# A linear-attention and long-convolution kernel: the filter's spectrum made straight on frequency partitions, one form of inverse tile, and a new order of all steps

## The chip, the cores and the metric

The kernel runs on one core of one Trainium2 chip. Its time is the device time of one execution in microseconds; the runs shown are three, and their median counts. A profile of one more execution shows where the time goes on the engines: PE (TensorE matmuls) and PEld (its weight loads), DVE (VectorE), ACT (ScalarE), POOL (GpSimd), SP (SyncE, which here only issues DMAs), and the DMA engines.

## The reference

Two parts follow each other. The first is linear attention with a feature map of exponentials, for 8 batches and 8 heads of 576 positions and width 64; the second takes its output, laid out as 8 x 576 x 512, projects it three ways, convolves one of the three with a filter along the sequence by FFT, multiplies, and projects once more.

```python
def phi(x):
    proj = np.einsum('bhsd,df->bhsf', x, w_phi)              # 64 -> 128 features
    proj = proj - np.max(np.abs(proj), axis=-1, keepdims=True)
    return np.concatenate([np.exp(proj), np.exp(-proj)], axis=-1)
q_p, k_p = phi(q), phi(k)
kv = np.einsum('bhsf,bhsd->bhfd', k_p, v)
z = np.sum(k_p, axis=2)
num = np.einsum('bhsf,bhfd->bhsd', q_p, kv)
den = np.einsum('bhsf,bhf->bhs', q_p, z)[..., None] + 1e-06
x = (num / den)                                              # then [8, 576, 512]

proj = x @ w_proj                                            # 512 -> 3 x 512
x1, x2, x3 = proj[..., :D], proj[..., D:2*D], proj[..., 2*D:]
X2 = np.fft.rfft(x2, n=576, axis=1)
H = np.fft.rfft(filter_fft, n=576, axis=0)[None]
y = x1 * np.fft.irfft(X2 * H, n=576, axis=1) * x3
out = y @ w_out
```

## The kernel before

All eight batches pass through the same chain of small steps, and every step is one method of a class. The order in which instructions are issued is written out by hand: the string `PLAN` (lines 31 to 193) is a list of words such as `Ie,0,2@2`; `run` (line 1061) walks through it and calls for each word the method of that name with the arguments that follow, and `@2` gives the PSUM bank (one of eight banks of 512 fp32 columns) that the step uses. Each engine executes its own instructions in the order of the list and waits for what they need; in the same way SP's and POOL's queues take their DMA issues in this order. Where a step has more than one possible engine, the word names it (`DVE`, `ACT`, `POOL`). `RING` gives how many buffers a tile has in turn.

The steps of one batch b, with v or m counting its four tiles:

- `load` (line 589) brings k, q and v of a batch into SBUF from POOL's queue; `trh` (601) transposes k and q by DMA from SP's queue. For batch 0, `loadh`, `pt` and `pte` do it by halves with PE. `w_load` (571) brings the weights, w_proj in three pieces.
- `Pk`, `Qn`, `Pkt`, `Qnt` (626 to 652): projections by w_phi; `maxk`, `maxq` and the like: their largest magnitude on DVE. `mhi`, `mlo`, `trm`, `trme` transpose the maxima of q.
- `ex`, `exkt`, `exqt` (685): exponentials on ACT; `Pq`: projection of q less its maximum; `em`, `vs` (742, 747): v scaled by the exponential of the maximum of k, mostly on POOL.
- `KV`, `KVe` (753): the sums over positions; `NE`, `rc`, `xn`, `NEt`, `rct`, `xnt` (771 to 813): numerator, denominator and quotient. `trx`, `trxt` (815): the quotient transposed by DMA from SP's queue into xT (for batch 0 three tiles go by PE, `ptx`).
- The forward transform of x runs before its projection: `f1`, `f2` (844, 850) fold the positions by sums and differences on DVE or POOL (both inputs in SBUF), `F` (855) multiplies by the tables D and Dt, `Fe` evicts into XF, `Xl` copies the last frequencies. `X2` (892) projects the spectrum, and `Y1` (899) multiplies it by the filter's spectrum in HTe, HTo and H5. `m3` (909) adds two of the products.
- `X1`, `X3` (940, 952): the other two projections, from xT; `X1e` evicts the first on ACT or DVE, `tm` (958) multiplies the second onto it on DVE.
- The inverse transform has two forms. `I` (966) makes even and odd halves with three matmuls each, in two banks; `Ie` (989) copies the even half to SBUF (es) on ACT, `Ip` and `Im` (999, 1002) form sum and difference on DVE (cv), and `ym` (1037) multiplies by x1s on POOL or DVE. `J` (1021) makes both final halves directly with five matmuls each, for which the table inv holds four more rows (`gen_neg`, `gen_ends`), and `yj` (1030) multiplies on DVE straight from PSUM. Of the 32 tiles 21 are made by I, 11 by J.
- `O` (1046): the output projection from yT, whose first step needs all four products of its batch; `Oe` (1052) evicts on ACT or DVE into one of four o buffers, `st` (1055) stores each in two halves, nearly always from SP's queue.

The filter's spectrum is made once, at the start, out of fl (512 rows, loaded in eight pieces) and flt (the 64 rows left): `fa` folds once on POOL in fp32, `rev` (497) reverses the partitions of two of the four results by an fp32 matmul with a reversed identity, `fb` (501) folds again on DVE into bf16, `Ff` (506) multiplies by D and Dt for each of four column blocks, with positions on the contraction side and channels on the partitions, `Ffe` scales and evicts, `Hl` gathers the last frequencies on ACT, `H` (532) turns the result by matmuls with the identity so that frequencies stand on the partitions, and `He` (538) evicts with signs and halves into HTe, HTo and H5. The copy `ft` is written for POOL, but the helper `copy` (293) knows only ACT and DVE and gives it to DVE.

`wz` (311) is a filler: two matmuls of zeros, 128 x 512, into a free bank. The list has ten of them, all ahead of the first X1.

`late` (275) closes the scratch space of the start, and the tiles T0 to T4, es, cv, yT and o are laid out in its place.

## Time and profile before

| | |
|---|---|
| median of three runs | 310.7 us (308.33 to 312.73) |
| span of the profiled execution | 311.6 us, the time used for it below |
| PE busy | 281.0 us, 90% |
| DVE busy | 268.6 us, 86% |
| ACT busy | 216.3 us, 69% |
| POOL busy | 203.8 us, 65% |
| mean granted clock of TensorE | 0.974 |
| read from and written to HBM | 33.75 MB, 9.44 MB |

The page gives no time around the span; the profiled execution is one among runs that lie between 308.33 and 312.73 us. In the rows, a line such as "L972 PE MATMUL" names the line of the code, the engine and the operation; "x126" is a count, and behind the bar stand the busy time of the group in us, the mean duration of one in ns, and the idle time of the engine ahead of the group with what ended it. Matmuls overlap in their pipeline, so that the duration of one is longer than the distance from one to the next; the chain of waits shows the latter (start, us, what).

### The profile page before, as it was taken

What the parts mean: (1) busy time and instruction counts of PE and PEld (TensorE: products, weight loads), DVE (VectorE), ACT (ScalarE), POOL (GpSimd) and SP (SyncE); (2) the same over time, 40 slices, a digit from 0 to 9 for tenths busy, and PEclk for the clock granted to TensorE, in tenths of its full rate; (3) what the DMA queues carried; (4) which work ended last, traced back from release to release, by engine and by line L of the source; (5) the groups of instructions that cost most, each with busy time, mean ns of one, the idle gap of its engine ahead of it and who ended that gap; (6) DMA issues with size and microseconds to landing.
All of it is one profiled execution on the core that took longest, in us unless ns stands there. A gap on an engine that the chain in (4) does not pass through costs nothing.

```text
span 311.6 us, 10240 instructions
## 1 busy us (share of the span) xinstructions
PE 281.0 (90%) x4331; PEld 205.3 (66%) x4360; DVE 268.6 (86%) x447; ACT 216.3 (69%) x345; POOL 203.8 (65%) x163
## 2 busy tenths in 40 slices
PE   1968977999999996999899799999999999999992
...
GB/s 162 235 203 159 136 202 193 105 190 133 91 164 204 94 110 170 116 160 107 114 198 82 131 160 153 172 175 160 84 117 4 56 93 69 19 110 21 1 115 192
DMA packets 72735, 40.20 MB, mean 129 GB/s; under 512 B 53040, under 2 KB 67504, under 8 KB 72688
## 3 DMA queue, kind: packets, MB, share of 16 engines
...
HBM read 33.75 MB, written 9.44 MB: 139 GB/s over the span
## 4 chain that ended last, share of the span: by engine, by line
PE 70%; DVE 12%; DMA 7%; ACT 5%; issue 3%; SPq 1%; POOL 0%; DVEq 0%; POOLq 0%
PE ps L919 16%; PE ps L897 10%; PE ps L1049 8%; PE ps L764 5%; PE ps L972 4%; PE ps L778 4%; DMA xT<-xn 4%; DMA out_dram<-o 3%; PE ps L1028 3%; PE ps L858 3%; PE ps L862 3%; PE ps L928 2%; DVE mq L707 2%; PE ps L665 2%; PE ps L638 2%
## 5 line engine op out<-in xcount | busy, mean ns | idle before, releaser
L919 PE MATMUL ps<-xT,wproj 128*128 128x256 bf16 x512 | 65.8, 275 | 4.3 <-DVE x1s L960 2.3
L919 PEld LDWEIGHTS <-wproj 128*128 128x128 bf16 x512 | 48.6, 98 | 14.5 <-issue 5.1
L707 DVE TENSOR_REDUCE mk<-ps 128x8 f32<-128x1024 f32 (+1 forms) x40 | 44.0, 1110 | 5.9 <-ACT HTo L295 2.2
L707 DVE TENSOR_REDUCE mq<-ps 128x8 f32<-128x1024 f32 (+1 forms) x40 | 44.0, 1110 | 5.5 <-PE ps L638 4.5
L749 POOL TENSOR_TENSOR vm<-vn,vm 128x1152 bf16<-128x1152 bf16 x14 | 30.4, 2178 | 18.2 <-ACT vm L743 18.2
L749 POOL TENSOR_TENSOR vp<-vn,vp 128x1152 bf16<-128x1152 bf16 x16 | 34.8, 2180 | 10.5 <-ACT vp L743 10.3
L911 POOL TENSOR_TENSOR T<-T,T 128x1024 bf16<-128x1024 bf16 x12 | 25.5, 2124 | 21.9 <-DVE T L907 21.8
L693 ACT ACTIVATE Ekp<-ps 128x1024 bf16<-128x1024 f32 x32 | 32.8, 1030 | 6.6 <-DVE mk L707 3.3
L1038 POOL TENSOR_TENSOR yT<-cv,x1s 128x576 bf16<-128x576 f32 x19 | 24.3, 1289 | 18.3 <-DVE x1s L964 12.8
L852 POOL TENSOR_TENSOR xf<-SD 128x512 bf16<-128x512 bf16 x27 | 31.2, 1170 | 6.7 <-DVE SD L846 5.3
L693 ACT ACTIVATE Ekm<-ps 128x1024 bf16<-128x1024 f32 x32 | 32.8, 1033 | 3.6 <-DVE mk L707 2.7
L693 ACT ACTIVATE Eqm<-ps 128x1024 bf16<-128x1024 f32 x32 | 32.9, 1034 | 3.1 <-PE ps L671 2.9
L1049 PE MATMUL ps<-wout,yT 128*128 128x512 bf16 x133 | 34.3, 385 | 0.7 <-issue 0.2
L693 ACT ACTIVATE Eqp<-ps 128x1024 bf16<-128x1024 f32 x32 | 32.5, 1031 | 3.4 <-PE ps L671 3.3
L846 POOL TENSOR_TENSOR SD<-xn 128x512 bf16<-128x512 bf16 x23 | 26.5, 1160 | 12.6 <-DVE xn L797 12.6
L897 PE MATMUL ps<-wproj,XF 128*128 128x512 bf16 x117 | 30.3, 380 | 0.7 <-issue 0.2
L295 ACT CAST x1s<-ps 128x512 bf16<-128x512 f32 (+1 forms) x30 | 16.0, 548 | 13.1 <-PE ps L928 8.4
L797 DVE TENSOR_TENSOR xn<-ps,r 128x512 bf16<-128x512 f32 x32 | 22.0, 689 | 1.1
L1049 PEld LDWEIGHTS <-yT 128*128 128x128 bf16 x144 | 13.4, 99 | 14.1 <-issue 0.6
L990 ACT COPY es<-ps 128x288 f32<-128x288 f32 x21 | 8.5, 404 | 20.3 <-PE ps L972 19.8
L960 DVE TENSOR_TENSOR x1s<-ps,x1s 128x512 bf16<-128x512 f32 x32 | 21.7, 683 | 0.6 <-ACT x1s L295 0.4
L778 PE MATMUL ps<-KVs,Eqp 128*128 128x65 bf16 x256 | 19.6, 192 | 2.2 <-DVE mq L707 0.6
...
## 6 DMA issues: line engine op xcount, KB each, us to landing
...
vn<-in_v_dram POOLq DMA_DIRECT2D x8, 576.0 KB, 7.5
kn<-in_k_dram POOLq DMA_DIRECT2D x7, 576.0 KB, 9.7
qn<-in_q_dram POOLq DMA_DIRECT2D x7, 576.0 KB, 6.6
wproj<-in_moe_w_proj_dram POOLq DMA_DIRECT2D x3, 512.0 KB, 5.9
...
```

Source lines behind the costliest of these rows:

```text
L693: self.nc.scalar.activation(e, p, AF.Exp, bias=0.0, scale=1.0 if g == "p" else -1.0)
L707: self.nc.vector.tensor_reduce(out=out, in_=src, axis=AX.X, op=ALU.max, apply_absolute_value=True)
L749: self.eng(eng).tensor_tensor(out=t[:, :, :, 0:64], in0=self.at("vn", b)[:, 2 * X:2 * X + 2], in1=t[:, :, :, 64:65].to_broadcast([128, 2, ...
L778: self.mm(self.pb(u, 65 * a, 65 * a + 65), E, KVs[:, u, v, s, :], start=(s == 0), stop=(s == 1))
L797: self.nc.vector.tensor_tensor(out=o, in0=n[:, :, :, 0:64], in1=self.at("r", 4 * b + v).to_broadcast([128, 2, 4, 64]), op=ALU.mult)
L846: self.eng(eng).tensor_tensor(out=o[:, :, 2 * i:2 * i + 2, :], in0=x[:, :, 0:2, :], in1=x[:, :, 2:4, :], op=ALU.subtract if i else ALU.add)
L852: self.eng(eng).tensor_tensor(out=o[:, :, 2 * i:2 * i + 2, :], in0=x[:, :, 0:4:2, :], in1=x[:, :, 1:4:2, :], op=ALU.subtract if i else ALU ...
L897: self.mm(self.pb(0), l, w[:, kt, 512:1024], start=(kt == 0), stop=(kt == 3))
L911: self.eng(eng).tensor_tensor(out=Y, in0=Y, in1=self.at(f"T{2 * e + 1}", b), op=ALU.add)
L919: self.mm(o[:, d], w[:, kt, f0 + 128 * m:f0 + 128 * m + 128], y[:, 1, ::-1, ::-1] if d else y[:, 0], start=(kt == 0), stop=(kt == 3))
L1038: self.eng(eng).tensor_tensor(out=self.at("yT", b)[:, m, 0:SEQ], in0=self.turn_of("cv", (b, m)).rearrange("p x h t -> p (x h t)"), in1=sel ...
L1049: self.mm(self.pb(0), y[:, kt, 128 * c:128 * c + 128], w[:, kt, :], start=(kt == 0), stop=(kt == 3))
```

## The change

What is computed stays the same. Five things differ.

1. **Filter spectrum.** `fa` now writes its folded rows in bf16 and nothing is reversed or folded a second time. Instead the table D gets a partner with reversed partitions, D2: `rv` multiplies D by a reversed identity in bf16 (two matmuls of 288 columns), and `rve` evicts it in two parts on DVE, one with the sign changed. `Hd` (in place of Ff, Ffe, Hl and H) makes each of the five tiles of the spectrum directly with frequencies on the partitions: three matmuls of 512 columns for each of four tiles, five for the last, whose tables zl2 and zlt are gathered by `zl` with ten small copies on POOL (over zeros that `zm` sets). `He` now also applies the scale HS.
2. **Inverse tiles.** `J`, `yj`, `gen_neg` and `gen_ends` are gone; all 32 tiles go by `I`, `Ie`, `Ip`, `Im` and `ym`. The table inv has 6 rows in place of 10. es and cv have three buffers in place of two.
3. **Engines.** Some steps change their engine, by the words of the list (steps before and after):

| step | before | after |
|---|---|---|
| f2 | DVE 5, POOL 27 | DVE 13, POOL 19 |
| f1 | DVE 9, POOL 23 | DVE 11, POOL 21 |
| ym | DVE 2, POOL 19 (and 11 yj on DVE) | DVE 4, POOL 28 |
| Fe | DVE 6, ACT 26 | DVE 11, ACT 21 |
| Oe | DVE 17, ACT 19 | DVE 9, ACT 27 |
| KVe | DVE 6, ACT 10 | DVE 9, ACT 7 |
| X1e | DVE 8, ACT 24 | DVE 5, ACT 27 |
| m3 | DVE 4, POOL 12 | DVE 3, POOL 13 |

4. **Order.** The whole list is written anew. Among other things the loads of q and k of batch 1 and their transposes come ahead of the load of v of batch 0, v of batch 1 and k of batch 2 ahead of the third piece of w_proj, and the filter's 64 rows (`fl_loadt`) behind the transposes of batch 1.
5. **Zero matmuls.** The method `wz` and its ten words stay; seven now stand at the head of the list, one ahead of `rv`, one in batch 2 and one between batches 2 and 4.

The diff, with most of the list left out:

```diff
@@ -24,172 +24,177 @@
 
 RING = {'Ekp': 4, 'Ekm': 4, 'Eqp': 3, 'Eqm': 3, 'vp': 3, 'vm': 3, 'r': 4, 'o': 4, 'kn': 2, 'qn': 2,
         'vn': 2, 'kT': 2, 'qT': 2, 'mk': 2, 'mq': 2, 'mh': 2, 'mT': 2, 'xT': 2, 'xTt': 2, 'KVs': 2,
-        'Fkp': 2, 'Fkm': 2, 'Fqp': 2, 'Fqm': 2, 'rt': 2, 'xnt': 2, 'es': 2, 'cv': 2, 'yT': 2}
+        'Fkp': 2, 'Fkm': 2, 'Fqp': 2, 'Fqm': 2, 'rt': 2, 'xnt': 2, 'es': 3, 'cv': 3, 'yT': 2}
 
 
 
 PLAN = """
-fl_load,2,1 cols_h loadh,q,0,0 zeros fl_load,3,0 gi_part loadh,q,0,1 ident fl_load,0,0 cols_i
-fl_load,1,0 gi_nr loadh,k,0,0 fl_load,1,1 w_load,phi loadh,k,0,1 cols_f load,v,0 fl_loadt ang,2
-gi_fr fl_load,0,1 gz,DVE ang,3 wz,10@0 fl_load,2,0 load,k,1 fl_load,3,1 wz,26@1 load,q,1 frac,3
-pt,q,0,0,0@0 gi_back ang,1 sin,3 pt,q,0,0,1@1 cols_m pte,DVE,q,0,0,0@0 ang,0 wz,13@2
...
+gi_part w_load,phi gz,DVE cols_h cols_i zeros fl_load,0,0 cols_f fl_load,2,0 wz,27@1 fl_load,0,1
+loadh,q,0,0 ident back,ACT wz,13@5 loadh,k,0,1 gi_nr loadh,q,0,1 wz,20@1 ang,3 wz,25@5 loadh,k,0,0
+fl_load,3,0 frac,3 fl_load,3,1 fl_load,1,0 ang,2 gi_fr wz,9@6 fl_load,2,1 ang,1 load,q,1
+fl_load,1,1 wz,1@1 wz,12@0 frac,2 pt,q,0,0,0@3 sin,3 trh,q,1,0 pt,q,0,0,1@0 pte,ACT,q,0,0,0@3
+trh,q,1,1 load,k,1 trh,k,1,1 trh,k,1,0 pte,ACT,q,0,0,1@0 zm,POOL cols_m frac,1 pt,k,0,1,0@2 sin,2
+ang,0 w_phi pt,k,0,1,1@3 Qn,0,1@4 sin,1 frac,0 pt,q,0,1,1@0 sin,0 Qn,0,0@6 load,v,0 pt,q,0,1,0@1
+pte,DVE,k,0,1,0@2 pte,ACT,k,0,1,1@3 maxq,0,1@4 fa,POOL,0 Pk,0,2@2 pt,k,0,0,0@4 pte,DVE,q,0,1,1@0
+pte,ACT,q,0,1,0@1 maxq,0,0@6 Qn,0,2@0 load,v,1 pt,k,0,0,1@5 Qn,0,3@6 pte,DVE,k,0,0,0@4 maxq,0,2@0
+Pk,0,0@0 pte,DVE,k,0,0,1@5 ex,k,p,0,2@2 maxq,0,3@6 ex,k,m,0,2@2 Qnt,0@4 ex,k,p,0,0@0 w_load,proj,2
+maxk,0,2@2 Pk,0,3@6 ex,k,m,0,0@0 ex,k,p,0,3@6 Pkt,0@2 exkt,m,0@2 maxqt,0@4 w_load,proj,1 mhi,0
+maxk,0,0@0 mlo,POOL,0 Pk,0,1@4 ex,k,m,0,3@6 exkt,p,0@2 maxk,0,1@4 maxk,0,3@6 ex,k,p,0,1@4
+maxkt,0@2 wz,10@0 rv@0 ex,k,m,0,1@4 load,k,2 one trm,0@7 trme,ACT,0@7 em,m,0,1 em,p,0,0
+rve,DVE,1@0 w_load,proj,0 em,m,0,0 fa,POOL,1 Pq,0,1@4 rve,DVE,0@0 Qn,1,0@2 em,p,0,1 vs,POOL,m,0,0
+fl_loadt Qn,1,3@0 ex,q,p,0,1@4 vs,DVE,p,0,0 Pq,0,3@6 ex,q,m,0,1@4 ex,q,p,0,3@6 vs,POOL,p,0,1
...
+xn,2,0@4 m3,POOL,1,1 exqt,p,2@2 Pq,2,3@0 Xl,DVE,1 f1,DVE,2,0,0 Pk,3,1@2 X2,1,4@4 KVe,DVE,2,1@6
+NE,2,2@6 maxk,3,1@2 wz,14@5 ex,q,m,2,3@0 f1,DVE,2,0,1 rc,2,2@6 ex,q,p,2,3@0 ex,k,p,3,1@2
...
+Pk,3,2@4 Ie,1,1@2 Pk,3,0@0 Im,1,1@2 ym,POOL,1,2 Ip,1,1@2 ym,POOL,1,3 ym,POOL,1,1 maxk,3,0@0
+ex,k,p,3,2@4 ex,k,m,3,2@4 X1,2,0@7 f1,POOL,2,1,1 maxk,3,2@4 X1,2,2@2 X1t,2@3 trh,q,4,0 X1,2,1@6
+st,SP,0,2,0 X1e,ACT,2,2@2 X1e,ACT,2,0@7 yt,ACT,1 ex,k,m,3,0@0 X1e,ACT,2,1@6 ex,k,p,3,0@0 Qn,3,3@4
+trh,q,4,1 X1te,DVE,2@3 f2,POOL,2,0,0 O,1,0@2 X3,2,0@3 Oe,ACT,1,0@2 O,1,4@7 maxq,3,3@4 em,p,3,0
+tm,2,0@3 Qnt,3@5 st,SP,0,0,0 Oe,ACT,1,4@7 Qn,3,1@3 f2,POOL,2,1,0 em,m,3,0 Pk,3,3@0 f2,DVE,2,1,1
...
+Ie,2,0@4 Ip,2,3@0 Im,2,3@0 st,SP,1,4,0 Ip,2,1@6 f1,POOL,3,1,0 ym,POOL,2,2 wz,26@0 Qn,4,1@0
...
+ym,POOL,7,0 Ie,7,1@4 Ie,7,2@0 ym,DVE,7,3 O,6,3@2 Ip,7,1@4 Ip,7,2@0 Im,7,1@4 ym,POOL,7,1
+st,SP,5,3,0 Oe,ACT,6,3@2 st,SP,6,3,1 st,SP,6,3,0 Im,7,2@0 O,6,0@4 Oe,ACT,6,0@4 st,SP,6,0,1
+st,SP,6,0,0 X3,7,2@0 tm,7,2@0 ym,DVE,7,2 O,6,1@6 Oe,ACT,6,1@6 O,7,2@2 yt,ACT,7 Oe,ACT,7,2@2
+O,7,4@4 Oe,DVE,7,4@4 st,SP,6,1,0 O,7,3@1 st,SP,6,1,1 st,SP,7,2,1 st,ACT,7,2,0 O,7,0@0 st,SP,7,4,1
+Oe,DVE,7,3@1 O,7,1@4 st,SP,7,3,0 st,ACT,7,4,0 Oe,DVE,7,0@0 st,SP,7,0,0 st,ACT,7,3,1 Oe,ACT,7,1@4
+st,ACT,7,0,1 st,SP,7,1,1 st,ACT,7,1,0
 """
...
@@ -239,7 +244,7 @@
         R("wout", [128, 4, 512], BF16)
         R("D", [128, 576], BF16)
         R("Dt", [128, 2, 576], BF16)
-        R("inv", [128, 10, 288], BF16)
+        R("inv", [128, 6, 288], BF16)
         R("HTe", [128, 4, 512], BF16)
         R("HTo", [128, 3, 512], BF16)
         R("H5", [128, 512], BF16)
@@ -320,10 +325,6 @@
         g.iota(self.part, pattern=[[0, 1]], base=0, channel_multiplier=1, **IOTA)
         g.iota(self.idx, pattern=[[1, 128]], base=0, channel_multiplier=-1, **IOTA)
 
-    def gi_back(self):
...
     def gi_fr(self):
         g, s = self.nc.gpsimd, self.scr
         self.fr = s.tile([128, 2, 2, 144], FP32, name="fr")
@@ -404,9 +405,9 @@
 
     def cols_h(self):
         v, c = self.nc.vector, self.at("cols")
-        v.memset(c[:, 16:18], 1.0)
-        v.memset(c[:, 18:19], -1.0)
-        v.memset(c[0:1, 16:17], 0.5)
+        v.memset(c[:, 16:18], HS)
+        v.memset(c[:, 18:19], -HS)
+        v.memset(c[0:1, 16:17], 0.5 * HS)
         v.memset(c[0:1, 17:19], 0.0)
 
     def cols_m(self):
@@ -484,87 +485,88 @@
     def ft(self, eng):
         self.copy(eng, self.f5, self.flt)
 
+    def back(self, eng):
+        self.copy(eng, self.rid, self.at("ident")[:, ::-1])
+
     def fa(self, eng, i):
         self.eng(eng).tensor_tensor(out=self.fs[:, 2 * i:2 * i + 2, :], in0=self.fl[:, 0:4:3, :],
                                     in1=self.fl[:, 2:0:-1, :],
                                     op=ALU.subtract if i else ALU.add)
 
-    def back(self):
...
-    def rev(self):
...
-    def fb(self, i):
...
-    def Ff(self, v):
...
+    def rv(self):
         for e in range(2):
-    def Ffe(self, eng, v):
...
+            self.mm(self.pb(e, 0, 288), self.rid,
+                    self.at("D")[:, 288 * e:288 * e + 288], True, True)
+
+    def rve(self, eng, s):
+        c = slice(144 * s, 144 * s + 144)
+        dst, src = self.D2.rearrange("p (e c) -> p e c", e=2)[:, :, c], self.db()[:, :, c]
+        if s == 0:
+            self.copy(eng, dst, src)
+        elif eng == "ACT":
+            self.nc.scalar.mul(dst, src, -1.0)
         else:
-            self.nc.vector.tensor_scalar(out=dst, in0=src, scalar1=HS, scalar2=None,
+            self.nc.vector.tensor_scalar(out=dst, in0=src, scalar1=-1.0, scalar2=None,
                                          op0=ALU.mult)
 
-    def Hl(self, eng):
-        src = self.HF[:, :, :, 128:160].rearrange("p v e (s x) -> p v e s x", s=2)
-        for d in range(2):
+    def zm(self, eng):
+        self.eng(eng).memset(self.zl2, 0.0)
+
+    def ends(self, x):
+        return x.rearrange("p (e c) -> p e c", e=2)[:, :, 128:160].rearrange(
+            "p e (s x) -> p e s x", s=2)
+
+    def zl(self, eng):
+        for i, t in enumerate((self.at("D"), self.D2)):
             for e in range(2):
-    def H(self, t):
...
+                x = self.ends(t)[:, e]
+                o = self.zl2[:, i, e, 64 * e:64 * e + 64].rearrange("p (d s x) -> p d s x", d=2,
+                                                                    s=2)
+                self.eng(eng).tensor_copy(o[:, 0], x)
+                self.eng(eng).tensor_copy(o[:, 1], x[:, ::-1])
+        x = self.ends(self.at("Dt")[0:64, 0])
+        o = self.zlt.rearrange("p (e d s x) -> p e d s x", e=2, d=2, s=2)
+        self.eng(eng).tensor_copy(o[:, :, 0], x)
+        self.eng(eng).tensor_copy(o[:, :, 1], x[:, :, ::-1])
+
+    def Hd(self, t):
+        D, D2, Dt, o, fs = self.at("D"), self.D2, self.at("Dt"), self.pb(0), self.fs
+        if t == 4:
+            self.mm(o, self.zlt, self.f5, start=True, stop=False)
+            for i in range(2):
+                for e in range(2):
+                    self.mm(o, self.zl2[:, i, e, :], fs[:, 2 * e + i, :], start=False,
+                            stop=(i == 1 and e == 1))
+            return
+        e, s = t // 2, t % 2
+        c = slice(288 * e + 160 * s, 288 * e + 160 * s + 128)
+        self.mm(o, Dt[0:64, 0, c], self.f5, start=True, stop=False)
+        self.mm(o, D[:, c], fs[:, 2 * e, :], start=False, stop=False)
+        self.mm(o, D2[:, c], fs[:, 2 * e + 1, :], start=False, stop=True)
 
     def He(self, eng, t, part):
         e, o, cols = self.at("HTe"), self.at("HTo"), self.at("cols")
         acc = self.pb(0)
 
         def mul(dst, src, c):
...
+            c = cols[:, c:c + 1] if isinstance(c, int) else c
+            if eng == "ACT":
+                self.nc.scalar.mul(dst, src, c)
             else:
-                self.nc.vector.tensor_scalar(
-                    out=dst, in0=src, scalar1=c if isinstance(c, float) else cols[:, c:c + 1],
-                    scalar2=None, op0=ALU.mult)
+                self.nc.vector.tensor_scalar(out=dst, in0=src, scalar1=c, scalar2=None,
+                                             op0=ALU.mult)
         if t == 0:
-            mul(e[:, 1 + part, :], acc, 16 if part else None)
+            mul(e[:, 1 + part, :], acc, 16 if part else HS)
         elif t == 1:
             mul(e[:, 3 * part, :], acc, 17 if part else 18)
             if part == 0:
...
+                mul(e[0:1, 1, :], self.pb(0, p1=1), 0.5 * HS)
         elif t == 2:
-            mul(o[:, 1, :], acc, None)
+            mul(o[:, 1, :], acc, HS)
         elif t == 3:
-            mul(o[:, 2 * part, :], acc, None if part else -1.0)
+            mul(o[:, 2 * part, :], acc, HS if part else -HS)
         else:
-            mul(self.at("H5"), acc, None)
+            mul(self.at("H5"), acc, HS)
 
@@ -1004,36 +1006,6 @@
 
-    def gen_neg(self, eng):
...
-    def gen_ends(self, eng):
...
-    def J(self, b, m):
...
-    def yj(self, b, m):
...
     def ym(self, eng, b, m):
         self.eng(eng).tensor_tensor(
             out=self.at("yT", b)[:, m, 0:SEQ],
@@ -1064,12 +1036,12 @@
         self.turn = s.tile([128, 9, 288], FP32, name="turn")
         self.fl = s.tile([128, 4, 512], FP32, name="fl")
         self.flt = s.tile([64, 512], FP32, name="flt")
-        self.fs = self.turn.rearrange("p a x -> p (a x)")[:, 0:2048].rearrange(
-            "p (a x) -> p a x", a=4)
-        self.fe = s.tile([128, 4, 512], BF16, name="fe")
+        self.fs = s.tile([128, 4, 512], BF16, name="fs")
         self.f5 = s.tile([64, 512], BF16, name="f5")
-        self.HF = s.tile([128, 4, 2, 288], BF16, name="HF")
-        self.HL = s.tile([128, 4, 2, 2, 32], BF16, name="HL")
+        self.rid = s.tile([128, 128], BF16, name="rid")
+        self.D2 = s.tile([128, 576], BF16, name="D2")
+        self.zl2 = s.tile([128, 2, 2, 128], BF16, name="zl2")
+        self.zlt = s.tile([64, 128], BF16, name="zlt")
         for word in PLAN.split():
             name, _, bank = word.partition("@")
             self.bank = int(bank) if bank else None
```

354 lines of the change are left out of this document (138 added, 216 removed).

## Prediction

> **What bounds the kernel now.** I read the page first, for the busy shares and the chain that ended last.
>
> ```profile
> span 311.6 us, 10240 instructions
> ...
> PE 281.0 (90%) x4331; PEld 205.3 (66%) x4360; DVE 268.6 (86%) x447; ACT 216.3 (69%) x345; POOL 203.8 (65%) x163
> ...
> PE   1968977999999996999899799999999999999992
> ...
> PE 70%; DVE 12%; DMA 7%; ACT 5%; issue 3%; SPq 1%; POOL 0%; DVEq 0%; POOLq 0%
> ```
>
> PE is busy for 281.0 of 311.6 us and carries 70% of the chain; DVE stands at 268.6, close behind. The row of slices puts nearly all of PE's idle time (30.6 us) into the first seven slices, one place in the middle (the 6 and the slices beside it) and the last slice. I cut the span accordingly and asked for the busy times of each stage:
>
> ```profile
> 0.00:56.00 56.00, 40.19 (x577) 26.83 (x581) 50.19 (x113) 42.80 (x68) 38.27 (x43) 0.92 1.04 182
> 56.00:112.00 56.00, 55.24 (x971) 41.71 (x974) 49.45 (x79) 44.76 (x70) 38.29 (x31) 0.99 0.92 139
> 112.00:120.00 8.00, 6.76 (x65) 4.96 (x66) 4.47 (x6) 5.44 (x9) 6.66 (x6) 1.00 0.93 147
> 120.00:128.00 8.00, 6.58 (x50) 3.89 (x52) 6.00 (x8) 3.55 (x8) 3.43 (x3) 0.79 0.57 125
> 128.00:288.00 160.00, 154.15 (x2545) 115.80 (x2558) 144.28 (x221) 115.27 (x182) 113.31 (x82) 1.00 0.67 110
> 288.00:311.60 23.60, 18.05 (x136) 12.11 (x135) 14.18 (x24) 4.43 (x9) 3.80 (x3) 0.95 0.39 102
> ```
>
> (Columns: PE, PEld, DVE, ACT, POOL busy, granted clock, DMA share, GB/s.) In the first 56 us PE idles 15.8 us while DVE works 50.2: this front is set by DVE and by what arrives by DMA. From 56 to 112 and from 128 to 288 PE is 98.6% and 96.3% busy against DVE's 88% and 90%: there, PE work taken out is time taken out, as long as DVE isn't last. From 112 to 128 lies one stall. So the change has to be priced in three places.
>
> **The change, part by part.** *Inverse tiles.* Eleven of the 32 tiles go from J (ten matmuls) to I (six). The chain has both:
>
> ```profile
> 237.56 0.73 PE ps L972 x6
> ...
> 299.56 1.23 PE ps L1028 x10
> ```
>
> 11 x (1.23 - 0.73) = 5.5 us of PE, in stages where PE is full. The other side of the exchange:
>
> ```profile
> L993 DVE TENSOR_TENSOR cv<-es,ps 128x288 f32<-128x288 f32 x42 | 17.3, 446 | 4.2 <-ACT es L990 3.8
> ...
> L990 ACT COPY es<-ps 128x288 f32<-128x288 f32 x21 | 8.5, 404 | 20.3 <-PE ps L972 19.8 <-DVE xn L797 0.3
> ...
> L1032 DVE TENSOR_TENSOR yT<-ps,x1s 128x576 bf16<-128x576 f32 x11 | 8.3, 753 | 0.7 <-PE ps L1028 0.2
> ...
> L1038 POOL TENSOR_TENSOR yT<-cv,x1s 128x576 bf16<-128x576 f32 x19 | 24.3, 1289 | 18.3 <-DVE x1s L964 12.8 <-DVE cv L993 5.4
> ```
>
> An I tile needs es on ACT and two half sums on DVE (17.3 / 42 = 0.41 each) and its ym product on POOL or DVE, where J had one yT product on DVE. DVE: 22 x 0.41 - 11 x 0.753 = +0.8; of the eleven products two go to DVE (+1.5) and nine to POOL (+11.6); ACT: 11 x 0.404 = +4.4. The path of one tile to O grows by about 0.40 + 0.82 + 1.29 - 0.75 = 1.8 us. I cost that at nothing where other steps stand between a batch's last product and its first O (13 to 22 in four batches); in batches 0, 4 and 5 there are only 5 to 7, and without cover they would pay 3 x 1.8 = 5.4, which the upper end of the coupling term below holds. In the tail the last tile's ym is on DVE and its I comes ahead of tm, so that the same two DVE instructions remain behind X3 as before.
>
> *Moved elementwise work.* In the written order DVE gets eight more f2, two more f1 and five more Fe, and gives eight Oe to ACT; three KVe more and three X1e fewer, all of them copies out of PSUM of about Oe's width, cancel.
>
> ```profile
> L852 POOL TENSOR_TENSOR xf<-SD 128x512 bf16<-128x512 bf16 x27 | 31.2, 1170 | 6.7 <-DVE SD L846 5.3 <-PE ps L897 0.5 <-DVE r L792 0.4
> ...
> L295 ACT CAST XF<-ps 128x576 bf16<-128x576 f32 x26 | 16.1, 642 | 7.4 <-PE ps L862 7.3
> ...
> L297 DVE COPY o<-ps 128x512 f32<-128x512 f32 x17 | 11.4, 684 | 5.9 <-DMA out_dram<-o 3.4 <-PE ps L1049 2.4
> ...
> L295 ACT COPY o<-ps 128x512 f32<-128x512 f32 x19 | 11.3, 594 | 11.3 <-PE ps L1049 9.8 <-issue 1.3
> ...
> L852 DVE TENSOR_TENSOR xf<-SD 128x512 bf16<-128x512 bf16 x5 | 4.3, 854 | 0.1
> ...
> L297 DVE CAST XF<-ps 128x576 bf16<-128x576 f32 x6 | 4.5, 752 | 0.9 <-PE ps L862 0.9
> ```
>
> Fe and Oe: 5 x 0.752 - 8 x 0.684 = -1.7. The ten f1 and f2 are the uncertain term, for the five f2 that DVE runs now differ among themselves:
>
> ```profile
> L852 DVE TENSOR_TENSOR xf<-SD x5: 415/425/2376, 49.2 to 272.8; 128x512 bf16<-128x512 bf16 x5
> ```
>
> Ten at the median 0.425 are 4.3 us, at the mean 0.854 8.5, all at the longest 23.8. I take 0.64, between median and mean, since four of the five lie near the median: +6.4. POOL loses 8 x 1.17 = 9.4 with the f2 and, with the 11.6 of ym and zl below, ends near 209; ACT gets 8 x 0.594 - 5 x 0.642 = +1.5 and ends near 222 with the es. Neither becomes the bound. [...]
>
> *Filter spectrum and front.* What goes and what stays:
>
> ```profile
> 17.35 1.20 DVE f L297
> ...
> 20.94 3.71 PE ps L499 x4
> ...
> 36.70 8.74 DMA xT<-xn
> ...
> 45.47 0.93 PE ps L919 x7
> ...
> 56.99 0.22 PE ps L536 x4
> ...
> 57.22 0.24 PE ps L858 x2
> ...
> 57.46 0.25 PE ps L862 x4
> ```
>
> ```profile
> 25.02 0.69 DVE L707 TENSOR_REDUCE mk<-ps 128x4 f32<-128x512 f32 x1 [0.75 <-PE ps L646]
> ...
> 25.63 2.34 DVE L502 TENSOR_TENSOR fe<-turn,ps 128x1024 bf16<-128x1024 f32 x2
> ```
>
> PE loses rev (3.71), four Ff (each like the L858 and L862 pair, 0.49, so 2.0) and five H (0.22 each, 1.1); it gets two matmuls of 288 columns for rv (0.24) and seventeen of 512 columns for Hd. Four of these take
>
> ```profile
> 126.99 0.86 PE ps L897 x4
> ```
>
> so 17 x 0.215 = 3.7, net -2.9. The front has 15.8 us of PE idle time to cover Hd; if that cover were gone, Hd would cost its 3.7. What counts is DVE: it loses the copy f (1.20; the step is written for POOL, but the helper sends it to DVE), both fb (2.34), one HF (as wide as XF's 0.752) and one HTe (as wide as o's 0.684), and gets two rve of 288 columns (0.41 each, by the half sums): -4.2. The 0.75 us that DVE waited behind rev goes too. So the front could be 5 us shorter.
>
> Against that stands the order of the loads. On POOL's queue q and k of batch 1 now come ahead of v of batch 0, and v of batch 1 and k of batch 2 ahead of the third w_proj piece; on SP's queue the four transposes of batch 1 move ahead of the filter's tail rows (fl_loadt).
>
> ```profile
> kn<-in_k_dram POOLq DMA_DIRECT2D x7, 576.0 KB, 9.7
> ...
> wproj<-in_moe_w_proj_dram POOLq DMA_DIRECT2D x3, 512.0 KB, 5.9
> ```
>
> Two 576 KB loads at the front's 182 GB/s are 6.5 us. The DMA share there is 1.04, so something lands later: KV of batch 0 waits for v, the first X1 for w_proj and for the transposed xT, which took 8.74 us to land with this traffic beside it. In return the loads are issued earlier, no longer behind products on POOL. Bounds for the front: -5 to +2. I take -3, nearer the sum of DVE, which worked through 50.2 of the 56 us. Behind X1, batch 0 has one more f2 and two more Fe on DVE, which the 3 us already allow for.
>
> zl is new on POOL: ten small copies and a memset, for which the nearest rows are
>
> ```profile
> L1018 POOL TENSOR_TENSOR inv<-inv 128x288 bf16<-128x288 bf16 x2 | 1.4, 744 | 0.0
> ...
> L731 POOL TENSOR_TENSOR mh<-mq,mh 128x36 bf16<-128x36 f32 x5 | 1.3, 255 | 2.7 <-ACT mh L727 2.7
> ```
>
> so 2.6 to 7.4 us; nearer the small one, 3. Behind it on POOL wait the issues of q of batch 2 and k of batch 3 and the first f1; POOL idles 56 - 38.3 = 17.7 us in the front, and Hd(4), which needs it, comes 30 steps later. Cost nothing; its whole 3 us, if F of batch 0 waits for that f1.
>
> *Zero matmuls.* The words of the change say that there are none; the diff keeps all ten wz steps. Seven now stand at the very start and fill PE while the loads are under way (nothing), one stands in the front, and two in the middle, in batches 2 and 4. Those two cost 2 x 2 x 0.215 = 0.9 if PE is full there. Taken.
>
> *Stores and queues.*
>
> ```profile
> 113.32 7.04 DMA out_dram<-o
> ```
>
> ```profile
> 120.46 0.69 DVE L297 COPY o<-ps 128x512 f32<-128x512 f32 x1 [2.99 <-DMA out_dram<-o]
> ```
>
> ```profile
> PE ps L858 <- DVE o L297: 2.4, 1, 2.4
> ```
>
> Stores of batch 0 stood on SP behind the five transposes of batch 2 and took 7.04 us to land; DVE's next eviction waited 3.0 us for the o buffer, PE 2.4 us, and the clock then fell to 0.79 for 8 us (1.7 us of PE time): 4.1 us. In the new order four of the eight stores of batch 0 go out ahead of these transposes (three before), but the second half of the very buffer that is wanted first stands behind one more transpose, of q of batch 4. It is wanted by an Oe on ACT now, and behind that queue Exp of k of batch 3 and the next Oe. I take half of the gain, -2; bounds -4.1 to +4.1. The ring of es and cv, 3 in place of 2, can only shorten waits; nothing is booked for it.
>
> *Coupling.* DVE: +0.8 + 1.5 - 1.7 + 6.4 - 4.2 = +2.8, to 271.4; PE: -5.5 - 2.9, to 272.6. Two engines of nearly equal load wait for each other more often than one in front; I charge half of DVE's increase, +1.4, from 0 to 5.
>
> *Sum.* 311.6 - 3 - 5.5 + 0.9 - 2 + 1.4 = 303.4 us of span. The profiled execution lies 0.9 us above the median of the runs (310.7); 303.4 - 0.9 = **302.5**.
>
> **Rivals.**
>
> *Everything lands.* Front -5, stall -4.1, no coupling: 311.6 - 5 - 4.6 - 4.1 - 0.9 = 297. For it: the front's DVE sum. Against it: the saturated DMA.
>
> *DVE takes the bound.* DVE reads two SBUF inputs in ten more instructions. POOL is busy 65% of the time with instructions of 1.17 us and more. If each of the ten waits one POOL instruction out, by the 1.17 of xf, they cost 15.9 in place of 6.4 and DVE stands at 281, where PE stands now; the gain in the inverse (4.6) and half of the front go: 302.5 + 4.6 + 1.5 = 308.6, 307 to 311. For it: the 2.376, and DVE's 90% between 128 and 288. Against it: four of five f2 met nothing. [...]
>
> *Slower: new gaps on PE that halve the clock.* The order is new everywhere, and one place where PE waits some 2.4 us for an eviction costs 4.1 us with the slow clock behind it, by the rows of the stall. The forecast gains 8.2, so two more such gaps than now undo it, and four, one for every second batch, give 302.5 + 16.4 = 319; 315 to 319. For it: DVE, now as loaded as PE, evicts every bank that PE fills. Against it: between 128 and 288 the present order has none (clock 1.00). [...]
>
> **How the numbers follow.** My forecast, 302.5 with its own range of 299 to 307: 0.45. Everything lands: 0.13. DVE takes the bound: 0.26. Gaps and clock: 0.16. The change not doing what it says concerns the wz steps alone and is inside the sum. A difference of 2% is 6.2 us, about what a measurement of this kernel tells from none (the runs shown go from 308.33 to 312.73). Faster than 304.5: three quarters of the forecast and the first rival, 0.34 + 0.13 = 0.47; above 316.9: 0.15, most of the last rival; the rest, 0.38, within. Range 297 to 313: it takes in the first three cases and leaves out the last.
>
> **What would show it.** Right: no matmul of L1028's kind, PE busy 271 to 274, DVE 269 to 274; the first X1 well ahead of 45.47 us; no DVE or ACT wait of 3 us for an o buffer; clock 0.98 or more from 56 us on. The DVE case: f1 and f2 on DVE with a mean near 1 us, DVE above 275, PE's waits naming DVE. The slow case: stages after 56 us with a granted clock under 0.95. The front is wrong if POOL's or DVE's scaling of v waits for the load, or the first X1 for w_proj. I would be wrong altogether if PE's idle time, 30.6 us now, is above 40.

## The result, and the profile after

The changed kernel is slower: 331.56 us (median of 4 runs, 329.26 to 332.8) against 309.62 (308.33 to 312.73), a ratio of 1.069 with a 95% interval of 1.059 to 1.078. The forecast was 302.5, its range 297 to 313. Medians here and below are over all runs of a kernel, ratios leave out runs that lie over 1.5% above that kernel's fastest. The page of the profiled execution first: busy times, slices, and the shares of the chain that ended last.

```profile
span 331.0 us, 10131 instructions
...
PE 283.6 (86%) x4257; PEld 202.9 (61%) x4287; DVE 282.9 (85%) x459; ACT 222.5 (67%) x357; POOL 209.1 (63%) x172
...
PE   7751509999998799999998999988999998999993
...
PEclk9655567999999599999999999999999999999997
...
PE 54%; DVE 19%; DMA 11%; SPq 5%; issue 4%; ACT 4%; POOL 1%; DVEq 0%; ACTq 0%; POOLq 0%
```

PE idles 47.4 us (30.6 before), 27.0 of them in the first 56 us (15.8 before), and its share of the chain fell from 70% to 54%. The same stretches as before:

```profile
0.00:56.00 56.00, 29.01 (x404) 19.68 (x406) 39.27 (x85) 30.27 (x43) 27.11 (x43) 0.63 1.13 172
56.00:112.00 56.00, 49.85 (x770) 35.07 (x775) 49.36 (x79) 40.57 (x67) 37.72 (x30) 0.97 0.83 122
112.00:128.00 16.00, 15.64 (x281) 12.17 (x281) 12.46 (x23) 12.11 (x18) 9.59 (x6) 0.87 0.99 152
128.00:288.00 160.00, 151.96 (x2385) 109.19 (x2402) 149.26 (x219) 123.01 (x200) 120.07 (x85) 1.00 0.62 109
```

In the first 56 us PE did 29 us of work in place of 40, VectorE 39 in place of 50, at a granted clock of 0.63 in place of 0.92. The loss is in the front. PE's longest waits of the whole execution (of the 6.9 us for qT, 3.2 come later, at 110 us), and then the chain's own pieces between 16 and 49 us (start, duration, what):

```profile
PE ps L633 <- DMA kT<-kn: 8.0, 1, 8.0
PE ps L673 <- DVE one L353: 7.5, 1, 7.5
PE ps L640 <- DMA qT<-qn: 6.9, 2, 3.7
```

```profile
16.03 2.39 SPq L604
18.47 7.29 SPq L604
25.86 7.55 SPq L604
33.46 15.60 DMA kT<-kn
```

Line 604 is the transpose of q and k of batch 1, which stand early on SP's queue now. The chain goes through their issues and the landing of the last, 15.6 us, from 16 to 49 us. SP's instructions for these transposes, a pair to a line, before and after (start, duration):

```profile
22.68 3.29 SPq L602 DMA_TRANSPOSE qT<-qn  x2
26.07 2.83 SPq L602 DMA_TRANSPOSE kT<-kn  x2
```

```profile
16.03 9.74 SPq L604 DMA_TRANSPOSE qT<-qn  x2
25.86 12.42 SPq L604 DMA_TRANSPOSE kT<-kn  x2
```

The w_proj products of the two kernels, before and after (count, shortest, median and longest in ns, start of the first and of the last):

```profile
L919 PE MATMUL ps<-xT,wproj x512: 269/273/421, 44.4 to 299.3; 128*128 128x256 bf16 x171
```

```profile
L921 PE MATMUL ps<-xT,wproj x512: 269/273/417, 63.8 to 319.6; 128*128 128x256 bf16 x171
```

The first X1 starts at 63.8 us in place of 44.4, which is the whole 19.4 us that the span grew by (the 45.47 of the prediction is the group of X1 behind its first matmul). From there to the end both take 267.2 us: the gain booked for the inverse isn't seen there either. PE's totals, 283.6 and 281.0, say little of the work: at a low clock the same work takes longer (sixteen matmuls of X1 take 3.52 us at 111.5 us, with a clock of 0.50, and 1.85 us at 63.8, with 1.00). A second suspect is on VectorE (start, duration):

```profile
23.58 7.98 DVE L352 TENSOR_TENSOR onex<-ident 128x36 bf16<-128x36 bf16 x1
```

The step `one`, with two small SBUF inputs, lasts 7.98 us; GpSimd runs four products without a pause beside it, from 22.85 to 31.5 us.

### The profile page after: what moved, and what is told of

It reads as the page before. It is cut to its first block, busy times and chain, and to the rows that moved or that the text cites. A ratio compares the mean times of both kernels' runs of the same rounds, so it can differ in the third digit from the quotient of the medians.

```text
span 331.0 us, 10131 instructions
## 1 busy us (share of the span) xinstructions
PE 283.6 (86%) x4257; PEld 202.9 (61%) x4287; DVE 282.9 (85%) x459; ACT 222.5 (67%) x357; POOL 209.1 (63%) x172
## 4 chain that ended last, share of the span: by engine, by line
PE 54%; DVE 19%; DMA 11%; SPq 5%; issue 4%; ACT 4%; POOL 1%; DVEq 0%; ACTq 0%; POOLq 0%
PE ps L921 13%; PE ps L899 8%; PE ps L1021 6%; SPq L604 5%; PE ps L974 5%; DMA kT<-kn 5%; DMA qT<-qn 3%; PE ps L766 3%; DVE mq L709 3%; DMA qn<-in_q_dram 3%; DVE mk L709 3%; PE ps L780 3%; DVE cv L995 2%; PE ps L667 2%; PE ps L930 2%
## 5 line engine op out<-in xcount | busy, mean ns | idle before, releaser
L1010 POOL TENSOR_TENSOR yT<-cv,x1s 128x576 bf16<-128x576 f32 x28 | 36.6, 1322 | 24.7 <-DVE cv L995 14.5
L751 POOL TENSOR_TENSOR vm<-vn,vm 128x1152 bf16<-128x1152 bf16 x16 | 34.4, 2154 | 6.7 <-ACT vm L745 6.7
L848 POOL TENSOR_TENSOR SD<-xn 128x512 bf16<-128x512 bf16 x21 | 24.0, 1160 | 21.6 <-DVE xn L799 20.5
L751 POOL TENSOR_TENSOR vp<-vn,vp 128x1152 bf16<-128x1152 bf16 x14 | 30.2, 2159 | 8.7 <-ACT vp L745 8.3
L913 POOL TENSOR_TENSOR T<-T,T 128x1024 bf16<-128x1024 bf16 x13 | 28.6, 2210 | 4.6 <-DVE T L909 4.4
L974 PE MATMUL ps<-inv,T 128*128 128x288 bf16 x192 | 27.9, 286 | 1.4 <-DVE cv L995 1.3
L995 DVE TENSOR_TENSOR cv<-es,ps 128x288 f32<-128x288 f32 x64 | 25.8, 443 | 0.9 <-ACT es L992 0.8
L854 POOL TENSOR_TENSOR xf<-SD 128x512 bf16<-128x512 bf16 x19 | 22.8, 1211 | 5.4 <-DVE r L794 3.5
L673 PE MATMUL ps<-mT,one 64*128 64x128 bf16 x256 | 17.8, 233 | 7.5 <-DVE one L353 7.5
L992 ACT COPY es<-ps 128x288 f32<-128x288 f32 x32 | 12.8, 404 | 15.7 <-PE ps L974 13.5
```

The source lines that it names most:

```text
L751: self.eng(eng).tensor_tensor(out=t[:, :, :, 0:64], in0=self.at("vn", b)[:, 2 * X:2 * X + 2], in1=t[:, :, :, 64:65].to_broadcast([128, 2, ...
L848: self.eng(eng).tensor_tensor(out=o[:, :, 2 * i:2 * i + 2, :], in0=x[:, :, 0:2, :], in1=x[:, :, 2:4, :], op=ALU.subtract if i else ALU.add)
L854: self.eng(eng).tensor_tensor(out=o[:, :, 2 * i:2 * i + 2, :], in0=x[:, :, 0:4:2, :], in1=x[:, :, 1:4:2, :], op=ALU.subtract if i else ALU ...
L913: self.eng(eng).tensor_tensor(out=Y, in0=Y, in1=self.at(f"T{2 * e + 1}", b), op=ALU.add)
L974: self.mm(self.pb(e, 0, 288), l, inv[:, 2 * e + i if i < 2 else 4 + e, :], start=(i == 0), stop=(i == 2))
L995: self.nc.vector.tensor_tensor(out=self.turn_of("cv", (b, m))[:, :, odd, :], in0=self.turn_of("es", (b, m)).rearrange("p (x t) -> p x t", ...
```

## The experiments

Two theories stood at first. **D**: the transposes of batch 1 go out among loads issued earlier than before, land late, and PE waits. **P**: GpSimd's unbroken products lock VectorE's two-input instruction out, and PE waits for `one`. A third, **C** (the zero matmuls, now at the start, no longer keep the clock up), was the way out if both failed; later came **Q** (D in a sharper form: it is the loads issued in front of the transposes that count). Ratios are to the kernel before, measured on the same chip.

**`one` early.**

```diff
-zeros ... loadh,q,0,0 ident back,ACT ... load,k,2 one trm,0@7
+zeros ... loadh,q,0,0 ident one back,ACT ... load,k,2 trm,0@7
```

> The changed kernel with one edit: the step `one` (a VectorE sum of two SBUF inputs, 7.98 us long at 23.58 us of the changed kernel's trace while GpSimd ran its products back to back, 0.17 us in the kernel before) stands right behind `ident`, before GpSimd has products. Theory P (the lock-out of VectorE by GpSimd lengthened the front): the wait of 7.5 us of PE for `one` goes and the time falls by 5 to 8 us, to 324 to 327. Theory D (the transposes of batch 1, issued among the loads and landing at 49 us, set the front): PE gets through Pq earlier but waits the longer for kT, and the time falls by 0 to 2 us, to 329.5 to 331.5.

328.68 us, ratio 1.066 (1.061 to 1.072): nothing that can be told from the change's 1.069. `one` was short, and the next two-input instruction took its place:

```profile
23.84 8.30 DVE L748 TENSOR_TENSOR vp<-vn,vp 128x1152 bf16<-128x1152 bf16 x1
```

**The DMA order of before, and both.** v of batch 0 goes ahead of q and k of batch 1; v of batch 1 and k of batch 2 behind the last w_proj piece; the transposes behind `maxkt`:

```diff
-load,q,1 ... trh,q,1,0 pt,q,0,0,1@0 ... trh,q,1,1 load,k,1 trh,k,1,1 trh,k,1,0 ... load,v,0 ... load,v,1
+load,v,0 fl_loadt ... load,q,1 load,k,1 ...
-maxkt,0@2 ... load,k,2 ... w_load,proj,0
+maxkt,0@2 trh,q,1,0 trh,q,1,1 trh,k,1,0 trh,k,1,1 ... w_load,proj,0 load,v,1 load,k,2
```

> The changed kernel with the DMA order of the kernel before: v of batch 0 ahead of q and k of batch 1, v of batch 1 and k of batch 2 behind the last w_proj piece, the four transposes of batch 1 behind Pkt of batch 0, the tail rows of the filter early. `one` stays where it is. Theory D: the transposes land within 3 to 5 us of their issue, PE's 8.0 us wait for kT goes, the first X1 starts near 52 to 56 us instead of 63.8 and the time falls by 8 to 12 us, to 320 to 324. Theory P: the 7.5 us wait for `one` is still there and what follows it is late anyway; the time falls by no more than 3 us.

> Both edits together. If P and D are both at work and add up: the first X1 near 45 to 48 us and a time of 312 to 317. If D alone: as the run with the DMA order alone, 320 to 324. If neither is the cause (a third theory C: PE's clock, granted at 0.50 from 8 to 40 us because the zero matmuls are no longer spread over the front): the first X1 stays past 55 us and the time above 322, with the granted clock still at 0.5 to 40 us.

329.78 us (1.066; 1.054 to 1.078) and, with both edits, 332.68 (1.079; 1.071 to 1.088). My form of D missed in both. The first run came out where P had put it (PE still waits 7.8 us for `one`), though `one` early had gained nothing by itself; the run with both came out where C had put it (the first X1 at 61.3 us, a clock of 0.54 from 8 to 40 us). But the transposes, though issued later, were as slow as ever. SP's instructions of the run with both edits, and what its DMA queues moved from 26 to 33 us (q0 the loads, q1 the transposes; packets, MB, share):

```profile
20.14 9.42 SPq L601 DMA_TRANSPOSE qT<-qn  x2
29.66 11.21 SPq L601 DMA_TRANSPOSE kT<-kn  x2
```

```profile
q0 software_dynamic: 1071, 1.11, 92.3%
q1 hardware_dynamic: 1072, 0.27, 29.0%
```

In the kernel before, where a pair took 3.29 and 2.83 us, the queues moved in these 7 us:

```profile
q1 hardware_dynamic: 3470, 0.86, 65.0%
q0 software_dynamic: 90, 0.09, 14.8%
```

All of w_proj, v of batch 1 and k of batch 2 (2.7 MB) had gone out between 17.1 and 23.4 us; the kernel before issues one w_proj piece there and the other four loads from 30 us on, between and behind GpSimd's products. That gave Q.

**GpSimd's products with pauses.** Only two load issues are put between them.

```diff
-load,k,2 one ... w_load,proj,0 ... vs,POOL,m,0,0 ... vs,POOL,p,0,1
+one ... vs,POOL,m,0,0 load,k,2 ... vs,POOL,p,0,1 w_load,proj,0
```

> The changed kernel with two load issues moved on GpSimd: k of batch 2 between the first and the second scaling of v, the last w_proj piece behind the third, so that GpSimd's products (2.38, 2.17, 2.17, 2.16 us back to back from 22.85 on) have pauses of 0.8 us in which GpSimd reads no SBUF. `one` stays. Theory P in its sharp form (VectorE's two-input instruction is held out for as long as GpSimd's products follow one another without a pause): `one` falls from 7.98 us to 5 us or less, PE's 7.5 us wait for it to under 5. If VectorE is held out for another reason (the DMA traffic, a late operand), `one` stays at 7 to 8 us.

```profile
25.31 0.17 DVE L349 TENSOR_TENSOR onex<-ident 128x36 bf16<-128x36 bf16 x1
...
26.34 1.35 DVE L748 TENSOR_TENSOR vp<-vn,vp 128x1152 bf16<-128x1152 bf16 x1
```

`one` takes 0.17 us in place of 7.98; it fell into a pause of 1.22 us in which GpSimd waited for an operand. So GpSimd's products beside it are what made it long. And the time is 333.61 us (two runs, 328.57 and 338.65; the profile is of the longer): PE waits 13.1 us for kT instead. P is right about the instruction; the time shows nothing of the 5 to 8 us that P had promised. Two of the loads stand later here, at 29.6 and 32.6 us, and the pairs of transposes are still issued in 9.65 and 11.34 us.

**The loads held back as well.** The run with both edits, and:

```diff
-w_load,proj,2 ... vs,POOL,m,0,0 ... w_load,proj,0 load,v,1 load,k,2 ... vs,POOL,p,0,1
+vs,POOL,m,0,0 w_load,proj,2 ... vs,POOL,p,0,1 w_load,proj,0 load,v,1 load,k,2
```

> The changed kernel with `one` early, the transposes and the first loads in the order of the kernel before (as in the run with both edits, which left the time at 332.7), and now also the loads of w_proj 2 and 0, v of batch 1 and k of batch 2 held back to where the kernel before has them: behind GpSimd's products. In the run before this one those 2.7 MB were issued from 17.1 to 23.4 us, ahead of the transposes and beside them; at 200 GB/s they fill the DMA engines for 13 us. Theory Q (it is the queue of loads in front of the transposes that makes them late, not the transposes' own place, and the pauses that the issues leave let VectorE through): each pair of transposes issues in 3 to 5 us in place of 9.4 and 11.2, the product of v on VectorE takes under 5 us in place of 8.7, the first X1 starts before 52 us and the time is 314 to 321. If Q is wrong (the order of compute in the front sets it): the first X1 stays past 57 us and the time above 324.

320.22 us (one run at 315.34, three from 320.21 to 320.33), 12 less than the 332.68 of the run it starts from, by moving four load issues. The two ran on different chips, on which the kernel before took 311.3 and 309.27:

```profile
20.50 5.11 SPq L601 DMA_TRANSPOSE qT<-qn  x2
25.70 2.84 SPq L601 DMA_TRANSPOSE kT<-kn  x2
```

The first X1 starts at 46.2 us (44.4 before). Q holds for the front. The order of compute there is still that of the changed kernel, so that this isn't what made it late. One thing moved along with the loads: their issues now stand between GpSimd's products, and VectorE's product of v took 1.36 us here. Pauses with loads still early had gained nothing in the run before; the loads held back without the pauses weren't tried.

**The same for batches 2 to 5.** First k of batches 3 to 5 and their transposes are held back, then the rest of that order:

```diff
 # first run, over the old front order
-load,q,2 ... load,k,3 ... w_load,out ... load,k,4 ... trh,k,3,1 trx,1,0 ... trh,k,3,0 ... trh,k,4,1 ... load,q,4 load,k,5
+load,q,2 ... w_load,out load,k,3 ... trx,1,3 trh,k,3,1 trh,k,3,0 ... load,q,4 load,k,4 ... load,q,5 load,k,5 ... st,SP,0,0,1 trh,k,4,1
 # second run, over the first
-load,q,4 load,k,4 ... mlo,POOL,2 ... load,v,3 ... load,q,5 load,k,5 ... vs,POOL,m,2,1
+vs,POOL,p,1,1 load,v,3 ... mlo,POOL,2 load,q,4 ... vs,POOL,p,2,1 load,k,4 vs,POOL,m,2,1 load,q,5 load,k,5
-trx,1,3 trh,k,3,1 trh,k,3,0 trxt,1 ... trh,q,3,1
+trx,1,3 trh,q,3,1 trxt,1 trh,k,3,1 trh,k,3,0
```

> The run with the old front order (320.2; it reached the last xn of batch 0 at 42.2 us, the kernel before at 41.5, the changed one at 59.8) and on top of it the same for batches 2 to 5: k of batch 3 loads behind w_out, k of batch 4 behind q of batch 4, k of batch 5 behind q of batch 5, and the transposes of k of batch 3 stand behind the four xT transposes of batch 1, that of k of batch 4 behind the second store of chunk 0, as in the kernel before. In the run without this PE waited 5.2 us for qT, 4.5 us for the tail transpose xTt and 1.9 us for more. Theory Q (transposes late beside loads issued early): these waits go and the time is 306 to 313. If the order of compute from batch 1 on is itself longer: the waits for DMA go, others take their place, and the time stays at 315 to 320.

321.55 us, 1.040 (1.033 to 1.048): a miss, by one wait made by the edit itself. q of batch 3 now stood behind k's transposes and beside loads of batch 4:

```profile
PE ps L637 <- DMA qT<-qn: 12.4, 3, 10.5
```

> The run with the loads held (321.6) with batch 3 put right: v of batch 3 loads behind the scaling of v of batch 1, q and k of batch 4 behind mlo and a scaling of v of batch 2, q and k of batch 5 behind another, and the second transpose of q of batch 3 ahead of those of k, as in the kernel before. In the run before, q and k of batch 4 were issued at 79.6 us, the transposes of k at 80.0 took 7.2 us, that of q at 90.1 landed 9 us later and PE waited 10.5 us for it, at a clock of 0.50. Theory Q: that wait goes, with 1 to 2 us of clock behind it, and the time is 307 to 313; what is left above 309 is the front's clock. If the order of compute from batch 1 on is longer by itself: 315 or more with no wait for DMA above 3 us.

316.86 us (316.13 to 318.53), 1.014 (1.006 to 1.022). PE's longest waits now:

```profile
PE ps L918 <- DMA xT<-xn: 2.7, 2, 2.5
PE ps L734 <- DVE mh L730: 2.5, 2, 1.3
PE ps L777 <- DVE cv L992: 2.2, 1, 2.2
PE ps L637 <- DMA qT<-qn: 1.8, 2, 1.4
```

The 10.5 us went, the ratio fell from 1.040 to 1.014, and the second outcome holds: no DMA wait above 3 us, and more than 315. So the order of loads and transposes makes most of the loss, 1.069 against 1.014, and what is left of the change isn't faster than the kernel before. Nearly all of that was gained in the front: whether the order of batches 2 to 5 adds anything to the 320.22 us (315.34 to 320.33) reached there, these runs don't show.

**Zero matmuls.** Five zero steps go back between the waits, over the run just told and over the changed kernel; and in the kernel before the front's zero steps go to the start:

```diff
 # over the restored order, and over the changed kernel
-wz,20@1 ... wz,25@5 ... wz,9@6 ... wz,1@1 wz,12@0 frac,2
+sin,1 wz,20@7 ... ex,k,p,0,0@0 wz,25@7 ... Pk,0,1@4 wz,9@7 ... trme,ACT,0@7 wz,1@5 ... ex,q,m,0,1@4 wz,12@5
 # over the kernel before
-gz,DVE ang,3 wz,10@0 ... wz,26@1 ... wz,13@2 ... wz,20@2 ... wz,9@4 ... wz,1@3 ... wz,12@3 ... wz,25@0 ... wz,14@6
+gz,DVE wz,10@0 wz,26@1 wz,13@2 wz,20@2 wz,9@4 wz,25@5 wz,14@6 fl_load,2,1 ... frac,3 wz,1@3 ... w_load,proj,1 wz,12@0
```

> The run with the order restored, and five of the seven zero steps of the start put back between the waits of the front (behind sin, the first Exp, Pk, trme and an Exp of q), where the kernel before has them. Theory C (in the kernel before, moving them to the start cost 8.8 us): the granted clock of the first 56 us rises from about 0.82 to 0.92 or more and the time falls by another 2 to 6 us, to 303 to 309. The prediction's term: no change against the order alone.

> The changed kernel with only these five zero steps put back between the waits. Theory C, if the clock itself is what lengthens its front: the clock of the first 56 us rises from 0.63 to 0.8 or more and the time falls by 4 us or more, to 327 or less. If the front waits for DMA whatever the clock: 329 to 333.

> The kernel before with the zero matmuls of the front where the changed kernel has them: seven steps (fourteen matmuls) in the first 8 us, one ahead of the first pt, one ahead of rev, none between Qn, Pk and Pq of batch 0. Theory C (the zero matmuls between the waits kept the clock up): the granted clock falls below 0.7 over the first 40 us (0.92 over 56 before) and the time rises by 2 to 6 us. The prediction's term: nothing, 308 to 312.

In the changed kernel: 319.14 us (1.021; 1.013 to 1.028) with the order restored, no faster than the 316.86 without, and 329.98 (1.054; 1.044 to 1.065) alone. The clock did rise. The first 56 us of the restored order, and of the same with the zeros spread:

```profile
0.00:56.00 56.00, 43.18 (x641) 28.77 (x642) 48.67 (x115) 44.89 (x69) 39.13 (x52) 0.82 1.09 184
```

```profile
0.00:56.00 56.00, 40.96 (x570) 26.64 (x572) 46.80 (x112) 43.23 (x67) 36.94 (x50) 0.91 1.07 182
```

With the clock at 0.91 in place of 0.82 less was done in 56 us, and the first X1 came 2.2 us later: a higher clock gained nothing here, though what the zero steps cost at their new places isn't told apart from it. In the changed kernel alone the clock went from 0.63 to 0.76 and the first X1 came 1.1 us earlier; the time lies where a front that waits for DMA had been put, and the ratio, 1.054 against 1.069 with intervals that overlap, leaves room for a small gain. So C explains at most a small part of the loss. In the kernel before, moving the zero steps to the start cost 1.029 (1.020 to 1.037; 318.13 us), with a clock of 0.79 over the first 40 us and 0.85 over 56. That is a miss of my term "nothing", and C's own marks, a clock under 0.7 and 2 to 6 us, are missed too (some 9 us); through what the move costs there, the trace doesn't settle. Its profiled execution is the fastest of the four, 2.8 us longer than that of the kernel before; its first X1 is 1.7 us late.

**The new DMA order alone, in the kernel before.**

```diff
-load,v,0 fl_loadt ... load,k,1 ... load,q,1 frac,3 pt,q,0,0,0@0 ... sin,3 pt,q,0,0,1@1
+load,q,1 cols_f fl_loadt ... gi_fr load,k,1 ... frac,3 load,v,0 pt,q,0,0,0@0 ... sin,3 trh,q,1,0 trh,q,1,1 trh,k,1,1 trh,k,1,0
-w_load,proj,2 KV,0,0@6 ... load,v,1 ... load,k,2
+maxq,0,1@0 load,v,1 ... w_load,proj,2 load,k,2 KV,0,0@6
```

> The kernel before, with only the DMA order of the changed one: q and k of batch 1 ahead of v of batch 0, v of batch 1 and k of batch 2 early, the four transposes of batch 1 right behind the first pt steps. The filter's loads, `one`, the zero matmuls and all compute stay. Theory D: the transposes take 10 to 15 us to land and the time rises by 5 to 12 us, to 315 to 322. Theories P and C: no change, 308 to 313.

318.94 us, 1.032 (1.021 to 1.042): the time that theory D had named, but not by its path. The pairs of transposes take 9.35 and 4.85 us to issue, and yet PE waits only 1.0 us for them and the first X1 is nearly on time (45.0 us); the profiled run lost most of its 2.6 us between 56 and 112 us, by what isn't shown.

**The two parts in the old order.** The inverse tiles alone, each J replaced in place; the filter path alone; both; and the inverse tiles with the products on VectorE:

```diff
 # inverse tiles (with the products on VectorE: ym,DVE,0,0)
-J,0,0@6 ... yj,0,0@6
+I,0,0@6 Ie,0,0@6 ... Ip,0,0@6 Im,0,0@6 ym,POOL,0,0
 # filter path
-rev@0 ... fb,0@0 ... fb,1@0 ... Ff,1@4 Ffe,DVE,1@4 ... trx,0,1 ... Hl,ACT H,0@4
+rv@0 ... rve,DVE,1@0 ... rve,DVE,0@0 ... trx,0,1 zl,POOL ... Hd,0@4
```

> The kernel before with only the inverse tiles changed: the eleven J become I (six matmuls, an es copy, two half sums and a ym product, ten of them on GpSimd), with es and cv three deep and the two preparing steps of J gone; everything else in the old order. By the prediction's terms: PE -5.5, VectorE +0.8 - 0.75 for the product that goes to GpSimd, so 2 to 5 us faster, 304 to 308. Rival (a path that grows from 1.23 + 0.75 to 0.73 + 0.4 + 0.82 + 1.29 us ahead of O, with GpSimd's product in it, makes PE wait for yT): 309 to 313.

> The kernel before with the inverse tiles and the filter's new path (reversed basis from one PE product, Hd in three or five matmuls, zl on GpSimd; reversal, second fold, spectrum copies gone), but in the order of the kernel before, loads, transposes and stores included: the new parts stand where the old ones stood. By the prediction's terms (inverse -5.5, front -4 of VectorE work, Hd 2.9 less on PE): 300 to 305. If the new order is what costs, this beats both kernels; if the new filter path itself is what lengthens the front (zl on GpSimd, Hd on PE), it is 310 or more and its first X1 later than 45 us.

> The kernel before with only the filter's new path, in the old order and with the J tiles as they were. In the run with both parts in the old order VectorE was busy 45.4 us of the first 56 in place of 50.2, as the prediction booked, and yet the last xn of batch 0 came at 41.7 us against 41.5. Theory F (the front is not set by VectorE's sum but by what lands by DMA; the VectorE work taken out was beside it): the time is 308 to 315, no faster than before. The prediction's own term (front 3 to 5 us shorter): 305 to 308.

> The run with the inverse tiles alone (323.2, GpSimd 216.1 us busy, PE waiting 3.1 us for yT, 2.4 for cv and 2.8 for vm), with the eleven new ym products on VectorE, so that GpSimd has no more work than in the kernel before. VectorE gets eleven of 0.75 us in place of the yj products it gave away. Theory G (GpSimd, made 11.6 us busier, was late with ym and with the scaling of v, and the cv ring made VectorE and PE wait for it): these waits go and the time falls by 4 us or more, to 309 to 319. If the longer path (es, two half sums, product) itself holds O up whoever multiplies: 321 or more.

Inverse alone 323.18 us (1.030; 1.020 to 1.041), filter alone 314.23 (1.015; 1.008 to 1.022), both 326.83 (1.045; 1.033 to 1.056), inverse with VectorE's products 317.94 (1.019; 1.009 to 1.030). Not one is faster than the kernel before. What the inverse took from PE is there, 33.5 us of matmuls down to 27.8, and so is what it gave to GpSimd. Groups of PE and of GpSimd, and PE's waits, with the inverse tiles alone:

```profile
L975 PE MATMUL ps<-inv,T 128*128 128x288 bf16 x192 | 27.8, 286 | 0.0
```

```profile
L1041 POOL TENSOR_TENSOR yT<-cv,x1s 128x576 bf16<-128x576 f32 x29 | 37.1, 1296 | 20.3 <-DVE x1s L967 11.5 <-DVE cv L996 8.7
```

```profile
PE ps L1052 <- POOL yT L1041: 3.1, 5, 1.1
PE ps L767 <- issue: 2.8, 1, 2.8
PE ps L634 <- DVE cv L996: 2.4, 2, 2.1
```

PE now waits for GpSimd's product five times, and 2.1 us for a half sum that itself stood behind a cv buffer a GpSimd product still held. With the products on VectorE the waits for GpSimd's yT go, and the ratio drops, but the intervals overlap: how much of the 3% is GpSimd's lateness stays open.

The filter path did take its work from VectorE (alone, 45.3 us busy in the first 56, 50.2 before), and the first X1 stayed at 44.0 us (44.4 before): that work had lain beside what sets the front.

A rival stays untried for all of these runs. Each of the six that change one or two things in the old order is slower, by 1.5 to 4.5%, whatever it changes. That order was written out by hand for its own timings, and a shift of any step may cost something by itself; no run here shifts the old order without changing what it does.

## Why the prediction was wrong

**Front: -3, measured +19.4.** This is the step that failed. The prediction saw all the moves ("the four transposes of batch 1 move ahead of the filter's tail rows", "q and k of batch 1 now come ahead of v of batch 0") and priced bytes for those who wait for v and w_proj. It wrote "in return the loads are issued earlier" as a gain, and of the transposes it counted only whom they now stand ahead of. It didn't price the transposes themselves beside a full queue of loads: 3 us a pair before, 10 to 12 after, and 15.6 to land, which put 8.0 us of waiting for kT and 3.7 for qT into PE's front. With the loads held back behind the transposes (and pauses between GpSimd's products) the first X1 was back at 46.2 us. The row of xT's 8.74 us landing under traffic, which it quotes, was such a price, and was used for xT alone. The two signs that it had named for a wrong front, the scaling waiting for v and the first X1 for w_proj, didn't come: the wait was elsewhere.

**VectorE's sum in the front: right (-4.2 booked, -4.9 measured with the filter path alone), and worth nothing.** The argument "nearer the sum of DVE, which worked through 50.2 of the 56 us" took a busy engine for the bound. With the filter path alone the work went and X1 didn't move.

**Inverse: -5.5 on PE, measured -5.6; the end didn't follow.** "PE work taken out is time taken out, as long as DVE isn't last" looked at one other engine alone. "I cost that at nothing where other steps stand between" and "neither becomes the bound" left GpSimd out: at 67% busy with the inverse tiles alone it was late where its product was needed or held a buffer (PE waited for yT five times, VectorE for a cv buffer twice), though how much of the loss these make isn't shown. The tile edit by itself is 3.0% slower in the old order; in the new order, with DMA put right, the whole is still 1.4% slower, where the terms behind the front came to 5 us of gain.

**f1 and f2 on VectorE: right side, too dear.** Booked 6.4 for ten; the groups stood at 6.2 + 4.3 us before and at

```profile
L848 DVE TENSOR_TENSOR SD<-xn 128x512 bf16<-128x512 bf16 x11 | 7.5, 708 | 0.1
L854 DVE TENSOR_TENSOR xf<-SD 128x512 bf16<-128x512 bf16 x13 | 6.7, 529 | 0.1
```

after: +3.7. VectorE's 282.9 (271.4 forecast) has 8.0 of `one` in it; with the order restored it is 278.4.

**Stores: the old stall went, and another came.** No engine waits for an o buffer to be stored any more. At 110 us PE waits 3.2 us for a transpose of q (issued at 98.9, landed 11 us later), and the clock is 0.50 from 112 to 116 us. zl came out at its 3 us (ten copies, most of 0.20, from 31.4 to 34.7 us). The two zero steps in the middle were not tried apart.

**The rivals.** "DVE takes the bound" had VectorE's wait for GpSimd right in kind, but not its place: it struck the step `one`, 7.8 us longer than in the kernel before, and not the f1 and f2 on VectorE, whose means (0.71 and 0.53 us) are far from the 1.6 it reckoned with. That each of the ten would wait out a GpSimd instruction was an estimate; it rested on the one xf of 2.376 us, which ran from 49.18 us beside a GpSimd product of 2.15 us, from 49.13; the other four took 0.42 to 0.63. The run in which `one` fell into a pause shows that it doesn't set the time. "New gaps on PE that halve the clock" came nearest in kind; its place (stages after 56 us), its cause (evictions by VectorE) and its price (319 at most) were wrong. The mark set for being wrong altogether, PE idle above 40 us, was passed with 47.4.

**Open:** what keeps the restored order 1.4% behind (its first X1 starts 1.8 us late, and its waits are all under 3 us); why moving the zero steps alone costs the kernel before 2.9%; and whether the 1.5% of the filter path and the 3.0% of the inverse tiles are their own or come of shifting the old order.
